# Three small slots of 12, 12 and 15 rows in place of 13 each, in a one-core channel-attention kernel

## The chip, the core and the metric

The kernel runs on one core of one Trainium2 chip. The metric is device time in microseconds (us), the median of several runs. A profile is one further execution, recorded by the hardware profiler; its span runs from the first to the last instruction.

## What is computed

```python
def reference(x, w1d):            # x: (1, 384, 384, 384) bf16, w1d: (1,) bf16
    g = jnp.einsum("bhwc->bc", x) / (H * W)
    s = jax.nn.sigmoid(g * w1d[0])
    return x * s[:, None, None, :]
```

This is the reference with k = 1 written out. The input has 147456 pixels of 384 channels. Each channel is averaged over all pixels, the mean goes through a sigmoid, and every pixel is multiplied with the resulting 384 numbers. No output can be written before the whole input has been read once. Input and output are 113 MB each, and the core's own memory holds a fraction of that.

## The kernel before, in words

The pixels are spread over 128 partitions, 1152 "rows" each; a row is 384 bf16 numbers, 768 bytes in each partition. A transfer of n rows therefore moves n x 768 bytes in each of 128 partitions. All rows live in one tile, `arena`, which has 275 row places in each partition.

**First half: the sum.** SyncE issues loads (`load`, line 231), and TensorE multiplies each row with a matrix of ones into one PSUM bank (`sum_rows`), which adds up the channels over all partitions and rows. Of the 1152 rows, 785 are *streamed*: read for the sum and read again later. The other 367 are *kept*. 71 of the kept rows stay in the arena as they are; the other 296 are packed by VectorE, four rows into three (`fold`), while ScalarE checks that the packing loses nothing. The packed rows fill the lower arena, so towards the end of the first half fresh rows pass through what is left: a stretch of `N_A` = 39 rows that begins at row `A` = 220. It is cut into three slots S1, S2, S3 (`SLOTS`, line 393). `BETWEEN` (line 403) says which slots are used between which folds: each use is a load into a slot, then its sum. Just before the sum is complete the three slots, and the scratch places U, V, T and Y (8 rows each), get the 71 rows that stay (line 437). ScalarE then takes the sigmoid into `s_bf` and copies it into PSUM (line 446).

**Second half: the output.** Everything is multiplied by `s_bf` (`scale`, line 451; VectorE, and GpSimd for three pieces) and written by `store` (line 462), issued on SyncE. The order is made while the kernel is being built: a planner (from line 566, its loop from line 688) keeps its own clock with assumed times for rows, transfers and VectorE operations, and records at each step what would be possible then. The rows that lie ready when the sum is done are entered in `landed` in lines 619 to 623: Y, Y, U, U, T, V in pieces of 4 and 8, then the first two slots. The third slot is scaled by GpSimd, in pieces of 4, 4 and 5 rows from row `A + 26` on (line 628), and those pieces are stored one by one. When a store has landed its places are free; the planner looks for the longest free run of rows (`runs`) and loads the next piece of the streamed rows into it, up to 48 rows, smaller ones only while little is queued. A loaded piece of more than 16 rows is scaled in parts. Between such pieces it unpacks the packed groups (`unfold`) in a fixed order (line 634), which needs a dozen VectorE operations for each 16 output rows. Where the runs of free rows have other lengths, the sizes and the order of all later loads and stores come out differently.

**Queues and waits.** Loads and stores share SyncE's queue, which issues in order: an issue that waits holds back all behind it. A load into a place waits for the store that emptied it; a store waits for the scale. Each transfer takes one of 24 semaphore lanes in turn, and waits for the transfer that had its lane 24 before (line 51).

Of the kernel before, what the change touches and what calls it, by code (L numbers as in the profile page):

```python
# [127 lines left out]
def kernel(  # L128
# [31 lines left out]
    A = V + PAIR  # L160
    N_A = 39
# [62 lines left out]
    def raw(a):  # L224

        return c_raw + (a - U if a < G0 else PAIR + a - V)
# [163 lines left out]
        lo, hi = i * BANK, min((i + 1) * BANK, PS * C)  # L390
        copy_bank(i, in_arena[:, lo:hi], bk[:, 0 : hi - lo], rows(A, PS), [("bank", i)])

    SLOTS = [(A + i, 13) for i in range(0, N_A, 13)]
    S1, S2, S3 = ([slot] for slot in SLOTS)

    HIGH = [(A - 48, 48)]
# [222 lines left out]

    for a, n, end in ((Y, 4, True), (Y + 4, 4, True), (U, 4, True), (U + 4, 4, True), (T, 8, True), (V, 8, True)):  # L620
        landed.append((KEPT, a, raw(a), n, end))
    for a, n in SLOTS[:2]:
        landed.append((KEPT, a, raw(a), n, True))


# [62 lines left out]
    while True:  # L688

        if dve_at <= now:  # L690
# [4 lines left out]
            if landed and (ahead < PENDING or not can):  # L695
                chunk, a, lo, n, end = landed.popleft()
# [13 lines left out]
        if alongside and alongside[0][0] <= now:  # L710
            _, chunk, a, lo, n = alongside.popleft()
            store(chunk, a, lo, lo + n)
            moves.append([now + LAT, n * ROW + PER_STORE, stored(a, n)])
        while waiting and waiting[0][0] <= now:
            _, n, then, chunk, a, lo, known = waiting.popleft()
# [12 lines left out]
        if bank_at is None and len(line) <= total - BANKS_AT and got and max(got)[0] >= PS * 4 // 3:  # L728
            a = max(got)[1]
# [9 lines left out]
        if got and todo < N_STREAM:  # L739
            n, a = max(got)  # L740
            n = min(n, CAP, N_STREAM - todo)
# [54 lines left out]
```

## Time and profile before

| | |
|---|---|
| Median of 3 runs | 721.59 us (720.78 to 722.45) |
| Span of the profiled execution | 719.6 us |
| Median less span | 1.99 us |
| Bytes read from and written to HBM | 190.41 MB, 113.25 MB |
| Transfers on SyncE's queue | 140 (81 loads, 59 stores) |
| First store issued | 269.92 us |
| Last matmul of the sum | ends at about 268.3 us |

The profile names engines PE (TensorE), DVE (VectorE), ACT (ScalarE), POOL (GpSimd) and SP (SyncE). Lines such as L456 are lines of the kernel; since `scale` and `store` are helpers, all scales have one line. In a row of stretches stand the stretch, its length, the busy time of each engine with its count of instructions, the granted share of TensorE's clock, the busy share of the 16 DMA engines and the GB/s that they moved. In a row of groups stand line, engine, operation, tiles and shape, then busy time, mean ns of one, and the idle time before them with what ended it. A row of the order in time has the start and the length in us first, and the idle time before in brackets. A transfer row has the size of one and the median us from issue to landing.

### The profile page before, as it was taken

The numbers are of one execution on the slowest core, as the hardware profiler recorded it, in microseconds if no ns is written. First come the engines' busy times: TensorE is split into PE (matmuls) and PEld (weight loads), VectorE is DVE, ScalarE is ACT, GpSimd is POOL, SyncE is SP. The second block draws the span as 40 slices with busy tenths as digits, with TensorE's granted clock in tenths as the row PEclk, the third lists the DMA queues.
The fourth block names the chain that finished last, engine by engine and source line by source line (L and its number), as shares of the span: only waits on it lengthen the run. The fifth ranks groups of instructions, "written<-read, shape, count | busy, mean of one in ns | idle before, by whom it ended". The sixth has DMA issues, their size and how long they took to land.

```text
span 719.6 us, 2061 instructions
## 1 busy us (share of the span) xinstructions
PE 210.5 (29%) x1202; PEld 0.3 (0%) x3; DVE 494.0 (69%) x471; ACT 115.7 (16%) x93; POOL 10.6 (1%) x7
## 2 busy tenths in 40 slices
PE   4678689888887770000000000000000000000000
PEld 0000000000000000000000000000000000000000
DVE  4600004887999819988999998999998985095500
ACT  3600003665777610002000000000000000000000
POOL 0000000000000005000000000000000000000000
PEclk9999999999999995555555555555555555555555
DMA  9999999999999979999999999999999999999997
GB/s 381 431 441 428 426 430 432 438 434 429 422 427 427 429 324 369 422 394 423 429 432 437 426 431 445 427 428 439 432 427 442 427 436 430 437 435 426 437 438 318
DMA packets 20173, 303.79 MB, mean 422 GB/s; under 512 B 2242, under 2 KB 2242, under 8 KB 6082
## 3 DMA queue, kind: packets, MB, share of 16 engines
q1 hardware_dynamic: 20160, 303.67, 99.0%
q8 instruction: 4, 0.07, 0.0%
q14 instruction: 7, 0.06, 0.0%
q10 hardware_dynamic: 2, 0.00, 0.0%
HBM read 190.41 MB, written 113.25 MB: 422 GB/s over the span
## 4 chain that ended last, share of the span: by engine, by line
DMA 61%; DVE 21%; ACT 6%; PE 5%; another core or an unknown queue 1%; SPq 0%; issue 0%; DVEq 0%
DMA arena<-in_x_dram 40%; DMA out_dram<-arena 21%; DVE arena L456 14%; ACT arena L313 6%; PE bank L242 5%; DVE arena L276 5%; DVE arena L282 2%; SPq L236 0%; ACT s_bf L443 0%; SPq L791 0%; DVEq L112 0%; SPq L106 0%
## 5 line engine op out<-in xcount | busy, mean ns | idle before, releaser
L456 DVE TENSOR_TENSOR arena<-arena,s_bf 128x4608 bf16<-128x4608 bf16 (+8 forms) x97 | 228.8, 2390 | 68.2 <-DMA arena<-in_x_dram 52.3
L276 DVE TENSOR_SCALAR arena<-arena 128x1536 uint16<-128x1536 uint16 (+2 forms) x247 | 145.3, 633 | 111.8 <-DMA arena<-in_x_dram 102.0
L242 PE MATMUL bank<-arena,ones 128*128 128x384 bf16 x1151 | 202.1, 336 | 48.9 <-DMA arena<-in_x_dram 48.9
L313 ACT ACTIVATE arena<-arena 128x3072 uint16<-128x3072 uint16 (+1 forms) x38 | 102.4, 2696 | 142.3 <-DVE arena L276 142.3
L282 DVE TENSOR_TENSOR arena<-arena 128x1536 uint16<-128x1536 uint16 (+2 forms) x114 | 121.0, 1061 | 5.2 <-PE bank L242 2.7
L529 PE MATMUL bank<-odd,ones 128*128 128x1 bf16 x1 | 0.2, 188 | 322.7 <-DVE odd L524 322.7
L456 POOL TENSOR_TENSOR arena<-arena,s_bf 128x1536 bf16<-128x1536 bf16 (+1 forms) x3 | 10.4, 3484 | 268.9 <-ACT bank L447 268.9
L386 ACT COPY arena<-bank 128x512 uint32<-128x512 uint32 (+1 forms) x7 | 4.0, 571 | 58.4 <-DMA out_dram<-arena 58.2
L456 DVE TENSOR_TENSOR arena<-arena,bank 128x1536 bf16<-128x1536 bf16 (+2 forms) x7 | 11.3, 1688 | 0.0
L242 PE MATMUL bank<-zeros,ones 128*128 128x384 bf16 x48 | 8.3, 326 | 0.0
L313 ACT ACTIVATION_READ_ACCUMULATOR arena<-arena 128x1 f32 x38 | 7.1, 186 | 0.0
L386 ACT COPY bank<-arena 128x512 uint32<-128x512 uint32 (+1 forms) x7 | 3.6, 566 | 0.0
L443 ACT ACTIVATE s_bf<-bank,w_sc 128x384 bf16<-128x384 f32 x1 | 0.6, 581 | 14.5 <-PE bank L242 14.5
L256 PE MATMUL bank<-arena,ones 128*128 128x384 bf16 x1 | 0.5, 478 | 6.9 <-DMA arena<-in_x_dram 6.9
L764 ACT ACT_TABLE_LOAD x1 | 1.3, 1283 | 0.7 <-PEq L780 0.7
L343 DVE TENSOR_SCALAR w_sc<-bank 128x1 f32<-128x1 f32 x1 | 0.2, 159 | 1.1 <-PE bank L338 1.1
L333 DVE MEMSET ones<- 128x128 bf16 x1 | 0.2, 165 | 1.0 <-SPq L106 1.0
L338 PE MATMUL bank<-w_bf,ones 1*128 1x1 bf16 x1 | 0.2, 181 | 2.1 <-DMA w_bf<-in_w1d_dram 2.1
L529 PEld LDWEIGHTS bank<-odd,ones 128*128 128x128 bf16 x1 | 0.1, 106 | 581.7 <-DVE odd L524 581.7
L533 DVE CAST odd_i<-bank 128x1 int32<-128x1 f32 x1 | 0.2, 159 | 0.3 <-PE bank L529 0.3
L447 ACT COPY bank<-s_bf 128x192 uint32<-128x192 uint32 x1 | 0.3, 323 | 0.0
L519 DVE TENSOR_REDUCE worst<-seen 128x1 f32<-128x38 f32 x1 | 0.2, 184 | 0.0
(8 smaller groups left out, 0.9 us busy)
## 6 DMA issues: line engine op xcount, KB each, us to landing
arena<-in_x_dram SPq DMA_DIRECT2D x15, 4608.0 KB, 35.4
arena<-in_x_dram SPq DMA_DIRECT2D x21, 1248.0 KB, 13.5
out_dram<-arena SPq DMA_DIRECT2D x7, 3072.0 KB, 33.1
arena<-in_x_dram SPq DMA_DIRECT2D x6, 3072.0 KB, 26.5
out_dram<-arena SPq DMA_DIRECT2D x4, 4608.0 KB, 39.2
arena<-in_x_dram SPq DMA_DIRECT2D x6, 2304.0 KB, 18.2
arena<-in_x_dram SPq DMA_DIRECT2D x3, 4512.0 KB, 27.0
out_dram<-arena SPq DMA_DIRECT2D x10, 1248.0 KB, 12.0
```

The lines of the kernel that those rows point to most:

```text
L242: return pe.add_instruction(mybir.InstMatmult(name=nc.get_next_instruction_name(), ins=[pe.lower_ap(rhs), pe.lower_ap(ones[:])], outs=[pe. ...
L256: return nc.tensor.matmul(acc, lhsT=ones[:], rhs=arena[:, i, :], start=first, stop=last)
L276: lambda: nc.vector.tensor_scalar(out=dst, in0=src, scalar1=s0, scalar2=s1, op0=op0, op1=op1),
L282: "DVE", lambda: nc.vector.tensor_tensor(out=dst, in0=a, in1=b, op=op), reads=reads, writes=writes
L313: lambda: nc.scalar.activation(out=y, in_=y, func=ACTF.Copy, accum_out=seen[:, 2 * k + i : 2 * k + i + 1]),
L333: fl.add("DVE", lambda: nc.vector.memset(ones[:], 1.0), writes=["ones"])
L386: "ACT", lambda: nc.scalar.copy(dst.bitcast(u32), src.bitcast(u32)), reads=reads, writes=writes
L443: lambda: nc.scalar.activation(out=s_bf[:], in_=acc, func=ACTF.Sigmoid, scale=w_sc[:, 0:1]),
L447: "ACT", lambda: nc.scalar.copy(s_ps.bitcast(u32), s_bf[:].bitcast(u32)), reads=["s_bf"], writes=["bank0"]
L456: lambda: vec.tensor_tensor(out=v, in0=v, in1=s[:, None, :].to_broadcast([P, n, C]), op=Op.mult),
L529: lambda: nc.tensor.matmul(votes, lhsT=ones[:], rhs=odd[:], start=True, stop=True),
L764: nc.scalar.preload_act_table(ACTF.Sigmoid)
```

## The change

The three slots get 12, 12 and 15 rows. GpSimd's pieces stay where they are, at `A + 26` and up; the third slot now begins at `A + 24`, two rows below them, and these two rows become a third piece that VectorE scales, with a store of their own.

```diff
-    SLOTS = [(A + i, 13) for i in range(0, N_A, 13)]
+    SLOTS = [(A, 12), (A + 12, 12), (A + 24, 15)]
     S1, S2, S3 = ([slot] for slot in SLOTS)
...
     for a, n, end in ((Y, 4, True), (Y + 4, 4, True), (U, 4, True), (U + 4, 4, True), (T, 8, True), (V, 8, True)):
         landed.append((KEPT, a, raw(a), n, end))
-    for a, n in SLOTS[:2]:
+    for a, n in SLOTS[:2] + [(A + 24, 2)]:
         landed.append((KEPT, a, raw(a), n, True))
```

Since S1, S2 and S3 stand in `BETWEEN`, the number of streamed rows that pass between the folds changes with them, and the very first stream load takes up the difference. The rest of the second half is planned anew from the changed runs of free rows.

## The prediction

> **What bounds the kernel now.** I read the page from its second section down: first whether any engine is full for long, then whether the transfers are.
>
> ```profile
> span 719.6 us, 2061 instructions
> PE 210.5 (29%) x1202; PEld 0.3 (0%) x3; DVE 494.0 (69%) x471; ACT 115.7 (16%) x93; POOL 10.6 (1%) x7
> DMA  9999999999999979999999999999999999999997
> GB/s 381 431 441 428 426 430 432 438 434 429 422 427 427 429 324 369 422 394 423 429 432 437 426 431 445 427 428 439 432 427 442 427 436 430 437 435 426 437 438 318
> q1 hardware_dynamic: 20160, 303.67, 99.0%
> ```
>
> The DMA row stands at 9 in 38 of the 40 slices, and the one queue that does the work fills 99.0% of the 16 engines' span. VectorE, the busiest engine, has 69%. So the time is bytes divided by rate, plus the few places where the rate falls: the first and the last slice, and slices 15, 16 and 18, which are the turn from summing to writing. A look at stretches shows how deep these places are.
>
> ```profile
> 55.00:110.00 55.00, 43.08 (x240) 0.00 (x0) 0.00 (x0) 0.00 (x0) 0.00 (x0) 0.94 1.01 435
> 210.00:255.00 45.00, 34.09 (x198) 0.00 (x0) 39.78 (x54) 31.26 (x22) 0.00 (x0) 1.00 1.01 427
> 260.00:270.00 10.00, 7.45 (x44) 0.00 (x0) 1.06 (x2) 0.90 (x2) 0.66 (x1) 1.00 0.57 236
> 278.00:318.00 40.00, 0.00 (x0) 0.00 (x0) 37.24 (x36) 0.00 (x0) 1.71 (x1) 0.50 1.01 393
> 280.00:290.00 10.00, 0.00 (x0) 0.00 (x0) 9.97 (x11) 0.00 (x0) 0.00 (x0) 0.50 1.02 371
> 310.00:320.00 10.00, 0.00 (x0) 0.00 (x0) 7.87 (x9) 0.00 (x0) 0.00 (x0) 0.50 1.00 369
> 318.00:340.00 22.00, 0.00 (x0) 0.00 (x0) 19.53 (x17) 4.00 (x7) 0.00 (x0) 0.50 1.01 427
> 340.00:590.00 250.00, 0.00 (x0) 0.00 (x0) 240.37 (x203) 0.00 (x0) 0.00 (x0) 0.50 1.01 433
> 710.00:720.00 10.00, 0.00 (x0) 0.00 (x0) 0.00 (x0) 0.00 (x0) 0.00 (x0) 0.50 0.54 229
> ```
>
> The last two numbers of a row are the DMA share and GB/s. Between 260 and 270 us the queue is empty because the first store needs the sum over everything; the change does not touch that dependence. Between 278 and 318 the engines count as full and yet move 393 GB/s where the next stretch has 427. That is 40 x (427 - 393) / 427 = 3.2 us, nearly all of it in two places: 10 x (427 - 371) / 427 = 1.3 us at 280 to 290 and 10 x (427 - 369) / 427 = 1.4 us at 310 to 320. I call these the two stalls. In them a packet takes longer than its size asks for; the trace does not name the reason. This is exactly the stretch in which the small slots are first emptied and refilled, so it is the one place where the change can do more than add transfers.
>
> **The change, part by part.** *Bytes.* Every one of 1152 rows per partition is read once for the sum, 785 are read again, 1152 are written: 3089 rows in both kernels. The three slots hold 39 rows either way. What streams through them between the folds is 129 rows in place of 130, and the odd row goes into an early load, which has 41 rows in place of 40. Bytes removed or added: none.
>
> *Number of transfers.* In the compiled order SyncE issues 145 of them in place of 140 (82 loads for 81, 63 stores for 59). The first half has 49 in both. The second half has the two-row store, and four more that the planner makes of its own accord, because other runs of rows come free together: for instance 12, 12, 13, 13 and 14 rows as five stores where before 24, 15, 16 and 16 went as four. What does one more transfer cost in a full queue? TensorE waits for each load while it sums, so its start times are landing times.
>
> ```profile
> 56.01 9.56 PE L242 MATMUL bank<-arena,ones 128*128 128x384 bf16 x48 [4.43 <-DMA arena<-in_x_dram]
> ...
> 99.48 9.64 PE L242 MATMUL bank<-arena,ones 128*128 128x384 bf16 x48 [2.91 <-DMA arena<-in_x_dram]
> ...
> 212.47 2.27 PE L242 MATMUL bank<-arena,ones 128*128 128x384 bf16 x13 [0.92 <-DMA arena<-in_x_dram]
> ...
> 258.84 2.27 PE L242 MATMUL bank<-arena,ones 128*128 128x384 bf16 x13 [1.31 <-DMA arena<-in_x_dram]
> ```
>
> From 56.01 to 99.48 lie 4 loads of 48 rows: 192 a + 4 f = 43.47 us, with a per row and f per transfer. From 212.47 to 258.84 lie 17 small ones of 202 rows together: 202 a + 17 f = 46.37. That gives a = 0.225 us and f = 0.05 us. The rates 435 and 427 GB/s of the same two kinds of stretch give 0.07. I take 0.06: 5 x 0.06 = **0.3 us**, with 0.25 and 0.35 as ends.
>
> A single transfer that nothing covers costs far more, and that is the other end.
>
> ```profile
> out_dram<-arena SPq DMA_DIRECT2D x6, 384.0 KB, 2.5
> arena<-in_x_dram SPq DMA_DIRECT2D x21, 1248.0 KB, 13.5
> out_dram<-arena SPq DMA_DIRECT2D x10, 1248.0 KB, 12.0
> arena<-in_x_dram SPq DMA_DIRECT2D x11, 768.0 KB, 11.4
> ```
>
> The four-row stores at the turn land 2.5 us after issue, of which 4 x 0.225 = 0.9 is data: 1.6 us each would be bare. But a 13-row load or store, 13 x 0.225 + 0.06 = 3.0 us of work, lands 12.0 to 13.5 us after issue, so some 9 us of other rows stand ahead of it. As long as that queue is there the 1.6 us lie beside other transfers. The two-row store takes two rows out of a later transfer, 0.45 us of data either way; its size is not in the trace as a store, so its price lies between 0 and 1.6 us, nearer to the 13-row rows, since three transfers are queued ahead of it.
>
> The Trainium skill, "DMA: Bandwidth & Descriptors", section "Anatomy of one DMA — SWDGE (gpsimd) path", fits a transfer as about 2.0 us plus its bytes over 436 GB/s, and its section "Bandwidth" advises batches of 1 MiB and more. By that rule, taken as if nothing overlapped, five more transfers and slots nearer to the 1 MiB mark speak against the change, by an estimated 10 us. The 17 small loads above land 2.7 us apart on average, with 0.05 us to spare over their bytes, so in a full queue this trace does not agree.
>
> *VectorE.* The scale of a slot changes length, and two rows are scaled by themselves.
>
> ```profile
> L456 DVE TENSOR_TENSOR arena<-arena,s_bf 128x4608 bf16<-128x4608 bf16 x25 | 63.5, 2551 | 3.7 <-DMA arena<-in_x_dram 3.7
> L456 DVE TENSOR_TENSOR arena<-arena,s_bf 128x4992 bf16<-128x4992 bf16 x12 | 32.9, 2752 | 2.6 <-DMA arena<-in_x_dram 2.6
> L456 DVE TENSOR_TENSOR arena<-arena,s_bf 128x768 bf16<-128x768 bf16 x1 | 0.6, 559 | 0.0
> L456 DVE TENSOR_TENSOR arena<-arena,s_bf 128x5376 bf16<-128x5376 bf16 x3 | 8.9, 2952 | 0.1
> DVE arena L456 <- DMA arena<-in_x_dram: 52.3, 12, 17.6
> ```
>
> 12 rows take 2.55 us, 13 take 2.75, 2 take 0.56: the row costs 0.20 and the instruction 0.15. Three more instructions are 0.45 us, and at the turn 12 + 12 + 2 rows take 5.66 us for 5.50. VectorE waits 52.3 us for loads in the output half, which is the cover: cost nothing. If the cover were gone, 0.45 us.
>
> *Order on SyncE.* Its queue is in order. The two-row store stands between the store of the second slot and the load that refills 8 rows of the third; behind it wait that load and the 12-row refill of the first slot. It waits for 0.56 us of VectorE, and the issue takes 0.33.
>
> ```profile
> 269.82 11.33 DVE L456 TENSOR_TENSOR arena<-arena,bank 128x1536 bf16<-128x1536 bf16 x7
> ...
> 269.92 8.92 SPq L466 DMA_DIRECT2D out_dram<-arena  x9
> 278.88 0.54 SPq L236 DMA_DIRECT2D arena<-in_x_dram  x1
> 279.74 2.19 SPq L466 DMA_DIRECT2D out_dram<-arena  x2
> 282.02 3.05 SPq L236 DMA_DIRECT2D arena<-in_x_dram  x2
> 289.51 0.34 SPq L466 DMA_DIRECT2D out_dram<-arena  x1
> ```
>
> Before, VectorE is through with the seven at 281.15, and the refill goes out at 282.02. With 12 + 12 the second store can go 0.4 us earlier, the two-row one follows 0.56 later, and the refill goes at about 282 as before. The rows up to the landing of the first slot's refill are 59 for 60. So the stretch moves by -0.2 + 0.1 us: nothing. In the second round the planner refills 10 and 12 rows where it refilled 8 and 13; what SyncE has in flight while it waits for the first slot's second store to land is 5 + 8 + 10 = 23 rows for 5 + 8 + 8 = 21, half a microsecond more cover. I take the two stalls as they are, 0 us, with -2.7 (both gone) and +1.4 (one more) as ends.
>
> *First half and end.* Slots of 12, 12 and 15 in the sum leave 32 rows in flight where 34 stood, 7 us, which covers a TensorE share of 15 x 0.17 us. The last load is 20 rows for 15, its scale about 4.1 us, and it lies under two stores of 47 and 36 rows, 18.7 us. The last store ends with the stream in both. Cost nothing.
>
> **Sum.** 719.6 + 0.3 = 719.9 us for the profiled execution. The median of the runs, 721.59, is 1.99 over the span; with the same distance, 721.9 us: +0.04%. A measurement of this kernel tells about 0.2%, 1.4 us, from no change.
>
> **Rivals.** *One more stall (slower).* Stalls appear only in the 40 us in which the pieces are 4 to 13 rows and loads and stores alternate; the stream of 427 to 435 GB/s before and behind has none. The change puts one more small piece, and one more turn of direction, into this stretch. Against it: the small pieces of the sum, loads alone, run at 427, and the other pieces grow (10 for 8). One more stall is 1.35 us: 721.9 + 1.35 = 723.2. It decides from 1.1 us on, that is, from four fifths of a stall.
>
> *Stalls gone (faster).* If they come from 8-row pieces with too little ahead, more cover of two rows ends the second one: 720.5, still within 0.2%. Both gone: 719.2. For it: the second stall sits where the flight is lowest. Against it: the first comes behind a row of 4-row stores that stays.
>
> *Bare transfers.* If the added transfers do not overlap, 5 x 1.6 = 8 us: 729.6. It needs a queue that runs dry at each; the 9 us ahead of each 13-row transfer speak against it. The Trainium skill's fit of 2.0 us a transfer, in the section named above, would make this its case.
>
> *The later order starves the queue.* VectorE is busy 240.37 of 250 us between 340 and 590, so a store planned too early holds SyncE. Against it: the rows ahead of such waits are 36 or more (8 us) in the new order by count. One dry spell costs the 1.6 us above: 723.5.
>
> That the change does not do what it says is excluded by the compiled order, in which the two-row store stands by itself.
>
> **How the numbers follow.** The forecast, stalls as they are, 0.47; one stall less, 0.13; both gone, 0.14; one more stall, 0.19; a dry spell, 0.05; bare transfers, 0.02. Faster by over 0.2%: 0.14. Within: 0.47 + 0.13 = 0.60. Slower: 0.26. The forecast's own range is 721.2 to 722.9. The range of 8 in 10 reaches down to 719.6, which leaves out most of "both gone", and up to 724.0, which leaves out the bare transfers and what is over one stall.
>
> **What would show it.** Right: the span near 719.9; the stretches beside 278 to 318 at 427 to 435 GB/s; queue packets up by 5 x 144 = 720 to 20880; the first store still at about 269.9; VectorE still waiting tens of microseconds for loads. A rate at 278 to 318 well off 393, up or down, is the stalls' rival; a slice under 420 behind 340 is the dry spell. Wrong would be a span that moves by more than 1.4 us with all rates unchanged, since then the sum has left out a term.

## The result, and the profile after

Eighteen runs of each kernel: 720.71 us after the change (719.93 to 722.26), 721.75 us before (720.78 to 723.66). The ratio is 0.9987 with a 95% interval of 0.9981 to 0.9993, that is -0.9 us or -0.13%. The forecast was +0.3 us. The sign is the other one, and 720.71 us lies below the range that the forecast gave itself, 721.2 to 722.9; the size stays within the 0.2% that the prediction called no change.

The profiled execution of the changed kernel took 720.62 us. Its page, the lines that answer to those of before:

```profile
span 718.8 us, 2072 instructions
PE 214.6 (30%) x1202; PEld 0.3 (0%) x3; DVE 494.1 (69%) x474; ACT 115.7 (16%) x93; POOL 10.6 (1%) x7
DMA  9999999999999979999999999999999999999997
GB/s 385 419 446 437 429 427 436 436 434 420 427 426 428 428 330 373 423 423 428 429 431 436 429 429 440 423 432 430 447 424 436 431 426 433 447 425 426 447 429 301
q1 hardware_dynamic: 20880, 303.67, 99.0%
```

The queue moved the same 303.67 MB in 20880 packets for 20160, and VectorE has three instructions more: both are what was worked out. What is new stands in slice 18 of the GB/s row: 423 where 394 stood. The view by stretches, with the DMA share and GB/s at the end of each row:

```profile
55.00:110.00 55.00, 43.15 (x240) 0.00 (x0) 0.00 (x0) 0.00 (x0) 0.00 (x0) 0.94 1.00 434
210.00:255.00 45.00, 34.33 (x199) 0.00 (x0) 38.77 (x52) 30.25 (x22) 0.00 (x0) 1.00 1.01 428
260.00:270.00 10.00, 7.54 (x45) 0.00 (x0) 1.34 (x2) 0.90 (x2) 0.94 (x1) 1.00 0.57 234
278.00:318.00 40.00, 0.00 (x0) 0.00 (x0) 37.66 (x37) 0.00 (x0) 1.42 (x1) 0.50 1.02 411
280.00:290.00 10.00, 0.00 (x0) 0.00 (x0) 9.97 (x12) 0.00 (x0) 0.00 (x0) 0.50 1.00 364
310.00:320.00 10.00, 0.00 (x0) 0.00 (x0) 8.99 (x10) 0.00 (x0) 0.00 (x0) 0.50 1.02 429
318.00:340.00 22.00, 0.00 (x0) 0.00 (x0) 21.90 (x19) 4.00 (x7) 0.00 (x0) 0.50 1.01 425
340.00:590.00 250.00, 0.19 (x1) 0.10 (x1) 235.76 (x203) 0.00 (x0) 0.00 (x0) 0.50 1.01 432
```

The first of the two stalls is still there, 364 GB/s for 371. The second is gone: 429 for 369 between 310 and 320 us. Over 278 to 318 us that is 40 x (411 - 393) / 411 = 1.75 us gained. Behind it 318 to 340 us gives back 0.1 us, and 340 to 590 us gives back 250 x (433 - 432) / 432 = 0.6 us, a figure that the rounding of the two rates leaves anywhere between 0 and 1.2. Together about -1.05 us, against -0.8 us between the two spans.

SyncE's issues in order of time, first at the turn, then around the second stall:

```profile
269.64 8.72 SPq L466 DMA_DIRECT2D out_dram<-arena  x9
278.40 0.74 SPq L236 DMA_DIRECT2D arena<-in_x_dram  x1
279.45 3.33 SPq L466 DMA_DIRECT2D out_dram<-arena  x3
282.88 1.92 SPq L236 DMA_DIRECT2D arena<-in_x_dram  x2
...
300.69 8.33 SPq L236 DMA_DIRECT2D arena<-in_x_dram  x4
309.06 5.19 SPq L466 DMA_DIRECT2D out_dram<-arena  x4
```

The same stretch of the kernel before:

```profile
301.78 9.24 SPq L236 DMA_DIRECT2D arena<-in_x_dram  x4
311.07 7.95 SPq L466 DMA_DIRECT2D out_dram<-arena  x4
```

The first store goes out at 269.64 us for 269.92 and the refill behind the two-row store at 282.88 for 282.02, so the turn costs less than a microsecond either way. At 300 us four loads go out one by one, with 5, 8, 8 and 13 rows before and 5, 8, 10 and 12 rows after, each into places that a store has to leave first. The four take 9.24 us before and 8.33 us after the change. This run of four loads is where the second stall lies, and the experiments turn on it.

### The profile page after: what moved, and what is told of

Same layout as the page of the kernel before. It is cut to its first block, busy times and chain, and to the rows that moved or that the text cites. A ratio compares the mean times of both kernels' runs of the same rounds, so it can differ in the third digit from the quotient of the medians.

```text
span 718.8 us, 2072 instructions
## 1 busy us (share of the span) xinstructions
PE 214.6 (30%) x1202; PEld 0.3 (0%) x3; DVE 494.1 (69%) x474; ACT 115.7 (16%) x93; POOL 10.6 (1%) x7
## 3 DMA queue, kind: packets, MB, share of 16 engines
q1 hardware_dynamic: 20880, 303.67, 99.0%
## 4 chain that ended last, share of the span: by engine, by line
DMA 70%; DVE 19%; PE 5%; ACT 2%; SPq 0%; another core or an unknown queue 0%; issue 0%; DVEq 0%
DMA arena<-in_x_dram 48%; DMA out_dram<-arena 22%; DVE arena L456 13%; PE bank L242 5%; DVE arena L276 4%; DVE arena L282 2%; ACT arena L313 2%; SPq L236 0%; ACT s_bf L443 0%; DVEq L112 0%; SPq L791 0%; SPq L106 0%
## 5 line engine op out<-in xcount | busy, mean ns | idle before, releaser
L242 PE MATMUL bank<-arena,ones 128*128 128x384 bf16 x1151 | 206.1, 341 | 44.8 <-DMA arena<-in_x_dram 44.4
L256 PE MATMUL bank<-arena,ones 128*128 128x384 bf16 x1 | 0.5, 478 | 6.7 <-DMA arena<-in_x_dram 6.7
```

What stands on the lines that cost most here:

```text
L242: return pe.add_instruction(mybir.InstMatmult(name=nc.get_next_instruction_name(), ins=[pe.lower_ap(rhs), pe.lower_ap(ones[:])], outs=[pe. ...
L256: return nc.tensor.matmul(acc, lhsT=ones[:], rhs=arena[:, i, :], start=first, stop=last)
```

## The experiments

The question is what ended the second stall. The theory that I came to is that the four loads are issued too late for the DMA engines that run ahead, and that the change issues them in better time; the rivals are the place of the pieces, their sizes and order, the two-row store, and the rows in flight as the prediction counted them.

Each kernel ran beside the kernel before on the same chip, so its ratio has its own control. One number is used throughout. The trace has, for every transfer, the time at which each of the 16 DMA engines reports its share done. *Margin* is the time from the issue of a load until the first of the 16 engines has reported the transfer ahead of it, the lowest such value of the loads issued between 300 and 313 us. In the kernel before, the 13-row load issued at 310.69 us has the first report of the one ahead at 312.70 us and the last at 316.79: margin 2.0 us, though the last engine has 6.1 us of work left. All results, the stall as GB/s between 310 and 320 us in the profiled execution:

| kernel | ratio to before, 95% | GB/s at 310 to 320 us | margin, us |
|---|---|---|---|
| before | 1 | 369 | 2.0 |
| changed | 0.9987 (0.9981 to 0.9993) | 429 | 3.5 |
| before again | 0.9993 (0.9984 to 1.0002) | 355 | 1.95 |
| before, shifted | 0.9998 (0.9989 to 1.0007) | 357 | 1.97 |
| changed again | 0.9985 (0.9976 to 0.9994) | 393 | 2.5 |
| changed, shifted | 0.9989 (0.9980 to 0.9998) | 428 | 3.2 |
| output half only | 0.9987 (0.9977 to 0.9997) | 427 | 2.7 |
| sum half only | 1.0019 (1.0010 to 1.0028) | 327 | 1.6 |
| no two-row store | 0.9991 (0.9983 to 1.0000) | 410 | 3.0 |
| eight-row refill | 0.9979 (0.9970 to 0.9989) | 422 | 3.0 |
| slots 13, 11, 2 | 0.9992 (0.9984 to 1.0001) | 370 | 2.2 |
| slots 14, 10, 2 | 1.0000 (0.9991 to 1.0009) | 425 | 2.9 |
| slots 12, 14 | 0.9993 (0.9984 to 1.0002) | 348 | 1.8 |
| refill behind two | 1.0042 (1.0030 to 1.0054) | 396 | 2.7 |
| refill behind one | 0.9997 (0.9988 to 1.0006) | 391 | 2.8 |
| loads held some | 0.9989 (0.9980 to 0.9998) | 411 | 2.3 |
| loads held long | 1.0015 (1.0006 to 1.0024) | 359 | 0.45 |

The ratio is one of medians; the last two columns are of a single execution, the profiled one. In these executions the time goes with the stall: the six with 348 to 370 GB/s (before, before again, before shifted, 13-11-2, 12-14, held long) have spans of 719.3 to 720.2 us, the four with 425 to 429 (changed, changed shifted, output half only, 14-10-2) 717.9 to 718.8. The sum half only is not among the six, since its edit has a cost of its own, as told below.

The packet records say what is slow in the stall. Outside the turn, before 250 us and behind 340 us, over 99 in 100 packets of one size take the same time in the kernel before: 234 ns for 8 rows, 347 for 12, 375 for 13. I call a packet *long* when it takes over 1.5 times the time of its size. Of the packets of 5 to 20 rows that start between 306 and 318 us, 33 of 631 are long in the kernel before, the longest with 1586 ns, and 5 of 677 in the changed one. What they take over the usual time comes to 1.26 us and 0.15 us for each of the 16 engines, and the difference, 1.1 us, is about the gain. So this stall is made of a few packets that take several times as long, and not of a rate that is lower for all.

**The kernel before, unchanged.** No edit.

> The kernel before once more, unchanged, for a second profile. Theory Q (queue): the stall at 310 to 320 us is made by the order, SyncE being held by the refill of the first slot with 21 rows queued, so it must show again: about 370 GB/s there, ratio 1.000 within 0.0007. Rival C (chance): the stalls fall where they will, and this profile has that stretch at 420 or more.

```profile
310.00:320.00 10.00, 0.00 (x0) 0.00 (x0) 7.87 (x9) 0.00 (x0) 0.00 (x0) 0.50 0.98 355
```

The stall is a property of the kernel and not of one execution. The ratio shows how far a kernel can stray from itself here: 0.0007, with an interval of 0.0009 to either side. Single ratios below are read with that in mind.

**Which half does it.** Two runs make the change in one half alone. In the first, the slots are 12, 12 and 15 rows for the sum, and the raw rows are loaded and written as 13s as before; in the second it is the other way round.

```diff
-    S1, S2, S3 = ([slot] for slot in SLOTS)
+    S1, S2, S3 = [(A, 12)], [(A + 12, 12)], [(A + 24, 15)]
...
-    for a, n in S2 + [(U, 8)] + S3 + S1 + [(V, 8), (Y, 8), (T, 5), (T + 5, 3)]:
+    for a, n in [SLOTS[1], (U, 8), SLOTS[2], SLOTS[0]] + [(V, 8), (Y, 8), (T, 5), (T + 5, 3)]:
```

> Slots of 12, 12 and 15 in the summing half alone; the output half is that of before. Theory Q: nothing changes, ratio 1.000, 310 to 320 us stays near 370 GB/s. Rival F (first half): the gain of 1.0 us comes from the summing half, ratio 0.9987, and the first store goes out about 0.3 us earlier.

```diff
-    for a, n in SLOTS[:2]:
+    for a, n in [(A, 12), (A + 12, 12), (A + 24, 2)]:
         landed.append((KEPT, a, raw(a), n, True))
```

> Slots of 13 in the summing half; the output half entered as 12, 12 and 2, so that its order is that of the changed kernel. Theory Q and rival S (sizes: pieces of 13 rows are worse than pieces of 12): the whole gain, ratio 0.9987, 310 to 320 us at 420 GB/s or more. Rival F: ratio 1.000 or, with five more transfers, 1.0004.

The stretches of the output half alone:

```profile
278.00:318.00 40.00, 0.00 (x0) 0.00 (x0) 37.00 (x37) 0.00 (x0) 1.62 (x1) 0.50 1.01 409
310.00:320.00 10.00, 0.00 (x0) 0.00 (x0) 8.13 (x9) 0.00 (x0) 0.00 (x0) 0.50 1.02 427
```

The output half alone has the whole gain: 0.9987, the ratio of the full change, to within the 0.001 of its interval. The sum half alone cannot be judged from its time, since the edit has a cost of its own: raw loads of 13 rows overlap two slots of 12, 12 and 15 and wait for both. The order in time of its SyncE and one stretch:

```profile
248.69 6.70 SPq L236 DMA_DIRECT2D arena<-in_x_dram  x8
270.86 3.43 SPq L466 DMA_DIRECT2D out_dram<-arena  x5
```

```profile
240.00:255.00 15.00, 9.79 (x57) 0.00 (x0) 13.15 (x18) 9.87 (x8) 0.00 (x0) 1.00 0.95 386
```

The first store leaves 0.9 us later than before, behind a hole in the loads that neither other kernel has (the one before moves 428 GB/s from 240 to 255 us). That is most of its 1.4 us. What the run does show: with the old sizes in the output half the stall is there, 327 GB/s.

**Is it the place?** The sizes change the addresses of the pieces too. Both kernels with everything in the arena moved by 256 bytes:

```diff
-    arena = pool.tile([P, ROWS, C], bf16, name="arena")
+    shift = pool.tile([P, 128], bf16, name="shift"); arena = pool.tile([P, ROWS, C], bf16, name="arena")
...
-    zeros = pool.tile([P, P], bf16, name="zeros")
+    zeros = pool.tile([P, 8], bf16, name="zeros")
...
-            fl.add("PE", lambda: add_held(zeros[:, None, :].to_broadcast([P, C // P, P])), reads=["zeros", "ones"], writes=["bank0"])
+            fl.add("PE", lambda: add_held(zeros[:, None, :].to_broadcast([P, C // 8, 8])), reads=["zeros", "ones"], writes=["bank0"])
```

> The changed kernel with its arena moved up by 256 bytes in each partition (the tile of zeros is cut to 16 bytes to make room), so that every even row place begins 256 bytes off a multiple of 512 where it began on one, and the other way round. Order and sizes as in the changed kernel. Theory P (a piece stalls when it begins at such a place; before, the second slot began at row 233): the stall comes to the changed kernel, 310 to 320 us at 370 to 400 GB/s, ratio 1.000. Theory E (pieces with an odd count of rows stall): no stall, 420 GB/s or more, ratio 0.9987.

> The kernel before with the same move of 256 bytes: the second slot (row 233) now begins on a multiple of 512 bytes, all even places do not. Theory P: the stall at 310 to 320 us changes its size, more pieces begin off 512 than before, ratio 1.000 to 1.002. Theory E: nothing changes, near 370 GB/s there, ratio 1.000.

The changed kernel, shifted, and then the kernel before, shifted:

```profile
310.00:320.00 10.00, 0.00 (x0) 0.00 (x0) 8.99 (x10) 0.00 (x0) 0.00 (x0) 0.50 1.03 428
```

```profile
310.00:320.00 10.00, 0.00 (x0) 0.00 (x0) 8.00 (x9) 0.00 (x0) 0.00 (x0) 0.50 0.97 357
```

Neither rate moved by more than 12 GB/s, so a shift of 256 bytes is not what decides. The slots of 12 and 14 below begin at rows 220 and 232 as in the changed kernel and have the stall (348): the place is not the cause.

**Is it the two-row store, the number of transfers, or the rows in flight?** With the slots of the changed kernel, GpSimd takes the whole third slot as 5, 5, 5, so that VectorE has no two rows to scale and no two-row store is left (138 transfers):

```diff
-    for a, n in ((A + 26, 4), (A + 30, 4), (A + 34, 5)):
+    for a, n in ((A + 24, 5), (A + 29, 5), (A + 34, 5)):
```

> The changed kernel without the two-row store: GpSimd scales all 15 rows of the third slot as 5, 5 and 5. The planner then refills 10 rows as one piece and keeps 35 rows queued when SyncE waits for the first slot's second store. Theory Q (too little queued at SyncE's low point): no second stall, 310 to 320 us at 420 GB/s or more, ratio 0.998 to 0.9987. Rival N (the two-row store itself is what helps): the gain goes, ratio 1.000. Rival S (pieces of 13 rows stall, of 12 do not): as theory Q.

The changed kernel with 8 rows in the refill that has 10. Two rows per partition are not read again, so two output rows hold other numbers, and 0.45 us of data is left out:

```diff
-                load(STREAMED, a, lo, lo + n)
+                skip = 2 if (a, n) == (A + 24, 10) and todo < 60 else 0
+                load(STREAMED, a + skip, lo + skip, lo + n)
```

> The changed kernel with one load cut from 10 rows to 8: the first refill of the third slot leaves out its lower two rows, so 21 rows are queued at SyncE's low point as in the kernel before; two output rows are then not those of the reference, and 0.45 us of transfer are missing. Theory Q: the second stall is back, 310 to 320 us at 370 to 400 GB/s, ratio 0.999 to 1.000 against before. Rivals S and N: no stall, 420 GB/s or more, ratio 0.998.

Other sizes for the pieces that VectorE scales first, in the output half of the kernel before. The line as it was, and the three lines that took its place in turn:

```diff
-    for a, n in SLOTS[:2]:
+    for a, n in [(A, 13), (A + 13, 11), (A + 24, 2)]:
+    for a, n in [(A, 14), (A + 14, 10), (A + 24, 2)]:
+    for a, n in [(A, 12), (A + 12, 14)]:
```

> The kernel before with its 26 VectorE rows stored as 13, 11 and 2 in place of 13 and 13: two-row store, 10-row refill and 145 transfers as in the changed kernel, but the first slot keeps 13 rows. Theory Q: 23 rows at the low point as in the changed kernel, no second stall, ratio 0.9987. Rival N: the same. Rival S: the 13-row pieces stall again, 310 to 320 us near 370 GB/s, ratio 1.000.

> The kernel before with its 26 VectorE rows stored as 14, 10 and 2: all counts and places even, 12 nowhere in the slots; 139 transfers, and 23 rows or more at SyncE's low point. Theories E and P: no stall, 310 to 320 us at 415 or more, ratio 0.9985 to 0.9990. A rival in which 12 rows alone are good: stall near 370, ratio 1.000.

> The kernel before with its 26 VectorE rows stored as 12 and 14 in place of 13 and 13: no two-row store, the third slot refilled with 8 rows, 21 rows at SyncE's low point as before, places 220 and 232. Only the counts and the place of the second slot are changed. Theories E and P: no stall, 310 to 320 us at 415 or more, ratio 0.9985 to 0.9990. Theory Q (low point) and rival N (two-row store): stall near 370, ratio 1.000.

The eight-row refill, then slots of 13, 11, 2, of 14, 10, 2 and of 12, 14:

```profile
310.00:320.00 10.00, 0.00 (x0) 0.00 (x0) 9.26 (x10) 0.00 (x0) 0.00 (x0) 0.50 1.03 422
```

```profile
310.00:320.00 10.00, 0.00 (x0) 0.00 (x0) 8.18 (x9) 0.00 (x0) 0.00 (x0) 0.50 0.98 370
```

```profile
310.00:320.00 10.00, 0.00 (x0) 0.00 (x0) 9.75 (x11) 0.00 (x0) 0.00 (x0) 0.50 1.02 425
```

```profile
310.00:320.00 10.00, 0.00 (x0) 0.00 (x0) 7.21 (x9) 0.00 (x0) 0.00 (x0) 0.50 0.99 348
```

Four simple causes fall. *The two-row store:* without it most of the stall stays away (410), and 13, 11, 2 has one and has the stall. *More rows in flight,* the prediction's reason: the eight-row refill leaves 21 rows in flight ahead of the last of the four loads, as in the kernel before, and shows no stall (with the 0.0006 for the data that it leaves out, its 0.9979 would be 0.9985, beside the 0.9987 of the changed kernel); 13, 11, 2 has 23 and shows it. *Pieces of 12 rows or even counts:* 12, 14 has only such, and stalls. *The count of transfers:* 144 (145 were expected), 139 and 144 in the last three, with no order in it. The medians do not order these three by the stall, and one does not fit: 14, 10, 2 has no stall in its profile and no gain, ratio 1.0000, while 12, 14 has the deepest stall and 0.9993. The profiled execution of 14, 10, 2 took 720.39 us against a median of 721.55, that of 12, 14 took 721.62 against 721.06, so one profile is not the mean of a kernel. What 14, 10, 2 loses in its other executions stays open.

**A longer flight by order.** In the kernel before, the last of the four loads, the 13-row refill, moves behind the stores of 13 and 20 rows that follow it, then behind the first of them only:

```diff
+    queue = [s for s in fl.steps if s.dma and s.eng == "SP"]
+    late, behind = queue[71], queue[73]
+    at, to = fl.steps.index(late), fl.steps.index(behind)
+    fl.steps.insert(to, fl.steps.pop(at))
```

The second has `queue[72]` in place of `queue[73]`.

> The kernel before with one transfer moved on SyncE: the second refill of the first slot (13 rows), whose wait holds the queue at 308 to 311 us, goes behind the two stores of 13 and 20 rows that are ready by then. Sizes and counts are those of before. Theory Q: more rows are queued at the low point (33 to 41 for 21), the second stall goes, 310 to 320 us at 420 GB/s or more, 1.0 to 1.4 us gained, ratio 0.9981 to 0.9986. Rival S: the sizes are the same, the stall stays, ratio 1.000.

> The kernel before, with the second refill of the first slot moved behind the one 13-row store that is ready before it can go (in the run above it stood behind 13 and 20 rows, which deferred its rows by 7 us and cost 2.6 us). Sizes and counts as before; 34 rows queued for 21 at the low point, and the refilled rows come 3 us later, of which VectorE has 2.4 us to spare soon after. Theory Q: the second stall goes or falls below 0.5 us, ratio 0.9985 to 0.9995. Rival S: it stays, ratio 1.000 to 1.002.

Behind two stores, the stretches around the stall and VectorE in order of time:

```profile
310.00:320.00 10.00, 0.00 (x0) 0.00 (x0) 7.99 (x9) 0.00 (x0) 0.00 (x0) 0.50 1.00 396
...
330.00:340.00 10.00, 0.00 (x0) 0.00 (x0) 9.93 (x12) 0.00 (x0) 0.00 (x0) 0.50 0.95 359
```

```profile
327.09 2.76 DVE L456 TENSOR_TENSOR arena<-arena,s_bf 128x4992 bf16<-128x4992 bf16 x1 [6.88 <-DMA arena<-in_x_dram]
```

Part of the stall goes (396 for 369), but the delayed load is missed 15 us later: VectorE waits 6.88 us for it, has nothing to store, and the DMA share between 330 and 340 us falls to 0.95. The sum is +3 us. Behind one store, 391 GB/s and a time that cannot be told from the kernel before. The gain that a fuller queue brought was spent elsewhere.

The packets show whose part of the stall went. In the kernel before, 26 of the 33 long ones have 13 rows, the size of the last load. Moved behind two stores, with a margin of 9.7 us of its own, that load has none among 123 packets; moved behind one, with 5.2 us, none among 161. The two 8-row loads, which stay where they were with margins of 2.7 to 2.9 us, have 20 and 23 long packets between 306 and 318 us, where the three profiles of the order before have 6, 15 and 16. With sizes and counts kept, the load that found more ahead of it lost its long packets, and the loads that did not kept theirs.

**Loads issued later, all else kept.** Up to here order or sizes changed together with the margin. The last three runs are of the changed kernel, and two of them hold two of the four loads back by a wait on VectorE; sizes, order, places and bytes stay.

```diff
+    queue = [s for s in fl.steps if s.dma and s.eng == "SP"]
+    done = [s for s in fl.steps if s.eng == "DVE"]
+    loads = queue[70:73]
+    at, to = fl.steps.index(loads[0]), fl.steps.index(queue[73])
+    fl.steps[at:to] = [s for s in fl.steps[at:to] if s not in loads] + loads
+    for load, after in [(70, 224), (71, 225)]:
+        queue[load].deps.append(done[after])
```

The longer hold has `(70, 225)` for `(70, 224)`; the control is the changed kernel again.

> The changed kernel, with two loads of the output half issued later by a wait on VectorE: the 8 rows of L71's second piece after the multiply that ends at 304.85 us (0.7 us later than in the changed kernel's profile) and the 10 rows behind them after the one that ends at 307.3 us (1.3 us later). Order, sizes, places and bytes stay. Theory A (a load loses time when it is issued less than about 3 us before the foremost of the 16 DMA engines has done what is queued ahead of it): the smaller of the two margins falls from 3.9 to about 2.6 us, so a part of the stall comes back: 310-320 us at 400 to 420 GB/s for 429, 0.3 to 0.6 us, ratio 0.9990 to 0.9996. Theory B (the stall belongs to the sizes and their order; a load may come any time before the last engine has done what is ahead): 425 GB/s or more, ratio 0.9987.

> As the run before, with both loads held to the multiply that ends at 307.3 us, the 8 rows 3.2 us later than in the changed kernel. The foremost engine is done with what is ahead of them at 308.03 us and the last one at 310.20 us, so the margin is 0.7 us to the first and 2.9 us to the last. Theory A: the stall is back in full, 310-320 us at 395 GB/s or less, 1 us or more lost, ratio 0.9998 to 1.0010. Theory B: nothing runs dry before 310.20 us, so 425 GB/s or more and ratio 0.9987.

> The changed kernel as it is, in the same rounds as the two with held loads, since they are read against it. Both theories: ratio 0.9987 to 0.9991, 310-320 us at 427 to 430 GB/s. If the ratio comes out at 0.9995 or more, the gain of the change is smaller than its first measurement says, and the two runs beside it tell nothing below 0.5 us by their times.

Held some, held long, and the control:

```profile
310.00:320.00 10.00, 0.00 (x0) 0.00 (x0) 8.60 (x9) 0.00 (x0) 0.00 (x0) 0.50 1.01 411
```

```profile
300.00:310.00 10.00, 0.00 (x0) 0.00 (x0) 9.13 (x7) 0.00 (x0) 0.00 (x0) 0.50 0.95 385
310.00:320.00 10.00, 0.00 (x0) 0.00 (x0) 8.48 (x9) 0.00 (x0) 0.00 (x0) 0.50 1.01 359
```

```profile
278.00:318.00 40.00, 0.00 (x0) 0.00 (x0) 36.88 (x37) 0.00 (x0) 1.82 (x1) 0.50 1.01 400
310.00:320.00 10.00, 0.00 (x0) 0.00 (x0) 7.81 (x9) 0.00 (x0) 0.00 (x0) 0.50 1.00 393
```

The long hold brings the stall back, 359 GB/s, and the kernel is slower than before the change: 1.0015, or 0.003 x 721.8 = 2.2 us over its control. That is more than either theory gave. The rates account for it: 10 x (421 - 385) / 421 = 0.9 us is lost between 300 and 310 us, where the share of 0.95 says that engines stand idle, and 10 x (429 - 359) / 429 = 1.6 us in the stall, both against the first profile of the changed kernel; against the 418 and 393 GB/s of the control they are 0.8 and 0.9 us. The order and the sizes are those of the changed kernel, so theory B falls: a later issue alone brings a stall back. Its margin of 0.45 us is far below the 2.0 of the kernel before, though, and there no engines stood idle ahead of the stall (423 GB/s and a share of 1.01 from 300 to 310 us), so this run does not show by itself that the kernel before stalls for the same reason. The short hold tests little: it gives 411 GB/s, in theory A's range, but in its control's profile the 8 and the 10 rows went out at 305.46 and 307.42 us, as late as here (304.98 and 307.45), and the two times cannot be told apart.

Two things keep theory A from being the whole answer. By its wording the late load itself should lose time. In the long hold the 8 rows with the margin of 0.45 us do so only at the front: their first report comes 3.0 us after that of the load ahead (308.18 to 311.19 us), for 1.9 us of bytes. On the last engine they and the 10 rows behind them end as soon as their bytes allow, and most of the loss falls on the 12-row load after them, whose margin is 4.0 us: it takes 2.0 us longer than its bytes (from 314.97 us, the last report of the load ahead, to 319.72: 4.75 us, where 12 x 0.225 + 0.06 are 2.76) and has 57 long packets. And the control has part of the stall in this execution (393 for 429 GB/s), with the margin at 2.5 us for 3.5, though its time over 11 runs repeats the gain. So the changed kernel is close to the edge and was over it in one of its three profiles.

## Why the prediction was wrong

**The step that failed** is "I take the two stalls as they are, 0 us". The first stayed; the second, 1.4 us in the prediction's count, is gone from two of the three profiles of the changed order and 393 GB/s deep in the third, and is present in all three of the order before (369, 355, 357). The means, 417 and 360, differ by 10 x (417 - 360) / 417 = 1.4 us; with the 0.3 us for the transfers that is -1.1 us, for -0.9 and -1.1 in the two measurements of the change.

**The rival was the right one, for half a reason.** "Stalls gone" named the second stall, the short flight as its reason, and 720.5 us; it came to 720.71, a fit that speaks for the stall and not for the reason. It got 0.13 of the chances, because I counted flight in rows (23 for 21) and found half a microsecond of it too little to matter. Rows were the wrong measure, as the eight-row refill and 13, 11, 2 show. The 16 engines do not work through a transfer in step. In the reports of the four loads the first engine is 3.1 to 4.1 us ahead of the last in the kernel before and 2.2 to 2.7 us in the changed one; so a count of rows in flight, an average over the engines, overstates what the first of them has left. Of 9 us of rows ahead that the prediction named for a transfer, the kernel before had 2.0 us left for the engine furthest ahead when the last of the four was issued.

**Where the margin grew** can be read from the landings. The 12-row store issued at 300.30 us in the changed kernel has landed by 308.67 us; its 13-row counterpart, issued at 301.04 us, landed at 310.68. The last load waits for that landing, and the loads ahead of it hold 23 rows for 21. What made the engines drift less apart is open: before, the load issued at 284.74 us widened the spread from 2.2 to 2.9 us, and its counterpart in the changed profile did not (1.8 and 1.7 us). In the control it did (2.1 to 3.0 us), and the control is the one with the smaller margin and part of the stall.

**What held.** Bytes, 145 transfers and 20880 packets came out as counted. The first store is 0.28 us earlier, the turn within a microsecond; the refill behind the two-row store, which the prediction left at about 282 us, went out at 282.88. VectorE's three instructions are covered, since it still waits tens of microseconds for loads in the output half; the view of its waits:

```profile
DVE arena L456 <- DMA arena<-in_x_dram: 72.2, 15, 18.9
```

The first half has no part in the gain that the run of the output half alone could show. No dry spell came in the later order: behind 340 us no slice but the last is under 420 GB/s. The 0.3 us for five transfers was not separated: the run with 138 transfers, seven fewer, gave 0.9991 with an interval that includes 0.9987. But the rival of bare transfers, 8 us, is out, and with it the estimate of 10 us by the fit in the Trainium skill, "DMA: Bandwidth & Descriptors", section "Anatomy of one DMA — SWDGE (gpsimd) path", read as if nothing overlapped. The section gives that fit for transfers issued from GpSimd; all of these are issued on SyncE, and no run here shows it for them.

**What stays open.** Shown: the gain is in the output half, at 310 to 320 us; the stall does not hang on places, on the two-row store or on rows in flight; a later issue of the same loads brings a stall back, and a fuller queue ahead of a load takes its long packets away. Over all seventeen profiles it is deep where the margin is 2.2 us or less (327 to 370 GB/s) and shallow or absent where it is larger (391 to 429), but not in strict order above that. Load by load there are 66 between 300 and 313 us; for each I count the long packets of its size from the first report of the transfer ahead to its own last report. The loads with margins up to 2.3 us have 6 to 25, those from 2.4 to 3.3 us have 0 to 23, and those above have 4 at most, but for one: the last load of the long hold, 57 with 4.0 us. So the margin goes with the stall and is not the whole of it. Why a packet takes several times as long, the trace does not show. The first stall was in every variant and was not studied; it begins with the first store of a slot, issued 2 us ahead of need behind eight small stores.

## What to carry to other kernels

Where the DMA queue bounds a kernel, look for stretches in which the busy share is full and the GB/s are not, and at the loads issued shortly before: two of the same loads, held until about 308 us, cost 2.2 us here, and moving one behind its stores only shifted the shortage to VectorE, 15 us on. Count what is queued ahead by the engine that will be done first and not by rows, for the 16 engines stood 2 to 4 us apart. And when a forecast takes a stall of unknown cause as fixed in the very stretch that the change rearranges, its disappearance deserves more than the 0.13 that it got here.

## What the runs showed of the hardware

- A full busy share is not a full rate: 1.00 stood beside 369 GB/s and 1.02 beside 429 in the same 10 us of the two kernels.
- The 16 engines that share a transfer report it up to 4.1 us apart (312.70 to 316.79 us in the kernel before), while the small stores at the turn are reported within 0.2 us.
- The loss in the stall is one of few packets: 33 of 631 took over 1.5 times the time of their size, up to 1586 ns, where a packet of 13 rows takes 375 ns outside the turn.
- The stall recurs at the same place over executions: in stretches of 2 us the lowest rate is 260, 284 and 266 GB/s in the three profiles of the order before, each between 312 and 316 us. In the long hold it lies at 314 to 318 us (287 and 253 GB/s). It does not go by addresses: 256 bytes of shift changed 369 to 357 and 429 to 428 GB/s.
